# The last stage of an FNet + MLP kernel: two chunks multiplied, turned and stored by halves of rows

## The chip, the cores and the metric

The kernel runs on 1 core of one Trainium2 chip. The metric is the device time of one execution in microseconds (us), the median of several runs. TensorE (PE) multiplies into PSUM, VectorE (DVE) adds and turns 32x32 blocks, ScalarE (ACT) copies and applies functions, GpSimd (POOL), SyncE (SP) and ACT issue the transfers (DMAs).

## The reference: a Fourier mixing layer and an MLP, added

```python
xn = _layernorm(x, axis=-1)                     # x: 1 x 2048 x 640, fp32
a = einsum("bsd,ed->bse", xn, dft_hid_re)       # hidden DFT, 640 x 640
b = einsum("bsd,ed->bse", xn, dft_hid_im)
y = einsum("ts,bse->bte", dft_seq_re, a) - einsum("ts,bse->bte", dft_seq_im, b)   # 2048 x 2048
h = gelu(einsum("bsd,df->bsf", xn, w1) + b1)    # 640 -> 1536
out = x + y + einsum("bsf,fd->bsd", h, w2) + b2
```

All inputs and the output are fp32.

## The kernel before

**Arithmetic.** Each fp32 operand is split into a high and a low part, and `product` (L297) makes one product of three matmuls: high by high (L300), high by low (L301), low by high (L302). A matmul takes a 128x128 weight block and 512 moving columns and adds into one PSUM bank of 128 partitions by 512 columns. There are eight banks in one tensor, `banks`. The large products are done by a seven-product scheme of the Winograd kind, whose partial sums are kept in PSUM and in SBUF.

**Stages.** The MLP comes first, then the Fourier part. There the 2048 rows are four blocks of 512 (`TB`), and the sequence DFT is applied before the hidden one. Stages are walked in a list (L1691 to 1715). An "s" stage applies the sequence DFT to one block and leaves sums `u`, `u1`, `u2`, `v`, `v1`, `v2` in SBUF. After two such blocks, ta and tb, a "y" stage (`hidden_entry`, L1645, and `hidden_beside`, L1510) multiplies the sums of the pair by the pieces of the hidden DFT matrix. The last pair is ta = block 1 and tb = block 2, and `last` is true in its stage.

**The entries of a "y" stage.** It has 21 entries, n = 0 to 20: seven products w, each in three parts u (pieces 0 and 1, 2 and 3, 4 of the 640 long sum). For each entry the loop writes down, in this order, the matmuls (`hidden_entry`), what must stand ahead (`pre`), the splitting of the moving operand of entry n + 3 (`form`: the high part on ACT at L186, the low part on DVE at L189), and the work listed for n in `post`. Each engine works through its own instructions in that order; the framework puts in the waits between engines. A semaphore of a finished transfer is used again for a later one, eight of them in turn for SP and ACT together and eight for POOL, and a later transfer is issued when the earlier one of its semaphore has landed.

**Columns.** 640 output columns are four groups q of 160 (`DQ`), one in each quarter of the partitions. Each 160 are five chunks of 32 (`B`). Columns 0 to 63 of a group come first, 64 to 127 from banks X and X+1 last (`k` = 2 and 3 at the end of the kernel), 128 to 159 are the odd chunk. A bank holds a chunk turned round: it is transposed in 32x32 blocks by DVE and added to what the MLP left (`turned`, L1295, then `add_turned`, L1305, whose adds are recorded at L463). `store` (L1276) writes a stretch of columns of a block to the output with four transfers, one for each q, in turn on the queues that it is given.

**The end of the last pair.** Product w = 6 (entries 18 and 19) first finishes bank VS with 15 matmuls, then adds to bank X with 15 and to bank X+1 with 15. Beside it, DVE does in this order: at n = 17 `v1` (reads banks X and X+1, 1024 columns), the two steps of `yb2` (turn `v1`, add it into `u2`'s place, store columns 64 to 127 of tb on SP and ACT), and `end`, which adds a turned chunk of the MLP's result (`last_columns`, L1575, made at n = 2) into bank X+1 only; at n = 18 `yb4` (turn bank VS, add, store columns 128 to 159 of tb on POOL). After the loop (L1718 to 1725) chunk 2 of ta is turned out of bank X into SBUF, added and stored on SP and ACT, and then chunk 3 is turned out of bank X+1 straight into the output tile (L1722) and stored likewise.

Of the kernel before, what the change touches and what calls it, by code (L numbers as in the profile page):

```python
# [17 lines left out]
B = 32  # L18
# [8 lines left out]
def kernel(  # L27
# [88 lines left out]
    def bank(k):  # L116
        return banks[:, k]
# [80 lines left out]
    def rows_of(ap, t):  # L198
        return ap[t * TB : (t + 1) * TB].rearrange("(n r) d -> r n d", r=B)
# [97 lines left out]
    def product(acc, wsp, msp, first, last, goes_on=False):  # L297

        (wh, wl), (mh, ml) = wsp, msp
        nc.tensor.matmul(acc, wh, mh, start=first, stop=False, skip_group_check=goes_on)  # L300
        nc.tensor.matmul(acc, wh, ml, start=False, stop=False, skip_group_check=goes_on)  # L301
        nc.tensor.matmul(acc, wl, mh, start=False, stop=last, skip_group_check=goes_on)  # L302
# [159 lines left out]
    def add(dst, a, b, op=ALU.add):  # L462
        nc.vector.tensor_tensor(dst, a, b, op=op)  # L463
# [809 lines left out]
            for k in names:  # L1273
                nc.sync.dma_start(part_of(t, k), sums[t, k])

    def store(t, src, c0, c1, *queues):  # L1276

        queues = queues or (nc.sync,)
        for q in range(Q):
            queues[q % len(queues)].dma_start(  # L1280
                rows_of(out, t)[:, :, q * DQ + c0 : q * DQ + c1], src[q * B : (q + 1) * B]
            )

    def reload(lo, w, which="xab"):
# [33 lines left out]
    turn(2, 1)  # L1318
    build(len(builds) - 1, "c")

    def use(acc, w, lo, a, c, first, last, goes_on=False):
        cols = slice(lo * P, (lo + 1) * P)
        product(acc, (w[:, 0, cols], w[:, 1, cols]), (a[:, 0, c % 2], a[:, 1, c % 2]), first, last, goes_on)

    X, Y, Z, US, VS = 0, 3, 5, 2, 7
    yo = {}
# [1 line left out]
    def beside(h, t, n):  # L1328
# [108 lines left out]
        else:  # L1437
# [15 lines left out]
            if n == 6 and p == 2:  # L1453
# [4 lines left out]
                        nc.sync.dma_start(yo[t][:, :, c0:c1], ys[k][t])  # L1458

                post.append(load_yo)  # L1460
            if n == 6 and second:

                def load_y4():
                    yo[t, 4] = A["y4"](f"y4_{t}")
                    nc.sync.dma_start(yo[t, 4], ys[2][t])

                post.append(load_y4)
# [24 lines left out]
    def load_g(b, i):  # L1492
        if i >= NW * ND:
            return
        w, c = G[i]
        n = GWIDE[w] * P
        places = A["g", b]
        k = i % len(places)
        if b < len(blocks) - 1 and w == NW - 1:


            k = (i - 2 if c == CHUNKS[1][0] else i) % len(places)
            if c in CHUNKS[0]:
                k = CHUNKS[0].index(c)
                places = {k: fr_tile((P, 6 * P), f"u{2 - k}_{sets[blocks[b]]}", f"gr{k}_{b}", F32R)}
        g = places[k][:, : 2 * n].rearrange("p (a b) -> p a b", a=2)
        GT[b, i] = g
        nc.sync.dma_start(g.bitcast(F32), wits[w][c])

    def hidden_beside(b, n):  # L1510
# [8 lines left out]
        def s(which, k):  # L1519
            return sums[(ta, tb)[which], k]  # L1520
# [20 lines left out]
        def to(dst, acc, name, then=lambda: None):  # L1541


            def f():
                add_turned(dst, turned(acc, name))
                then()

            return f
# [21 lines left out]
            return f  # L1570

        def out_b(k):
            return lambda: store(tb, columns(k), 2 * k * B, 2 * (k + 1) * B, *(((nc.gpsimd,), (nc.sync, nc.scalar))[k] if last else ()))

        def last_columns():  # L1575

            A["end"] = A["rt2"][:, 0, 0, 0]
            nc.vector.transpose(A["end"].rearrange("p (n i) -> p n i", i=B), ya[:, :, 3 * B : 4 * B])

        yb1, yb2 = in_two(0), in_two(1)  # L1580
        yb4 = to(yo[tb, 4], vs, f"yb4_{tb}", lambda: store(tb, yo[tb, 4], 4 * B, DQ, *((nc.gpsimd,) if last else ())))
# [63 lines left out]
    def hidden_entry(n, b, w, u):  # L1645
        last = b == len(blocks) - 1
        where = (X, Y, Z, X, Z, X, X)[w]

        def use_g(acc, j, pos, first, stop, goes_on=False):
            r, k = (n - u + (pos // 2)) % 3, pos % 2  # L1650
            a = A["as"][:, r]
            use(acc, GT[b, w * ND + pos], j, a, k, first, stop, goes_on)

        def wide(j, pos):
            use_g(bank(where + j), j, pos, w < 3 and pos == 0, pos == ND - 1, w > 2)

        mine = (2 * u, 2 * u + 1) if u < 2 else (4,)
        if w == 6 and last:

            if u == 0:  # L1660
                for pos in range(ND):
                    use_g(bank(VS), 2, pos, False, pos == ND - 1)
                for pos in range(ND):
                    wide(0, pos)
            elif u == 1:
                for pos in range(ND):
                    wide(1, pos)
# [24 lines left out]
    for kind, what in stages:  # L1692
# [20 lines left out]
            X, Y, Z = Y, Z, X  # L1713
        if kind == "y":
            put_off.clear()


    t = blocks[-2][1]  # L1718
    for k in (2, 3):
        d = yo[t][:, :, k * B : (k + 1) * B]  # L1720
        if k == 3:
            nc.vector.transpose(d, bank(X + 1).rearrange("p (n i) -> p n i", i=B))  # L1722
# [34 lines left out]
```

## Time and profile before

| what | value |
|---|---|
| median of 3 runs (lowest to highest) | 852.09 us (851.99 to 852.13) |
| span of the profiled execution, first to last instruction | 849.9 us |
| instructions | 10599 |
| mean granted TensorE clock | 0.998 |
| PE, DVE, ACT, POOL busy | 841.9, 686.7, 368.6, 67.7 us |
| DMA | 166.53 MB, mean 196 GB/s |

The profiled execution is told of by its span alone; the three times are of other executions and lie 2.2 us above it, which is what stands outside the first and the last instruction. Times in the views count from the start of the span. In a timeline row stand the start, the duration, the engine, the line of the kernel, the operation, what is written and read, the shape and a count; "q" behind an engine means that its sequencer issues a transfer, and a bracket tells how long the engine had been idle and what ended that. "PEld" is the weight load of a matmul. The end of a matmul is modelled.

### The profile page before, as it was taken

The page shows a single profiled execution, that of the slowest core. Times are in us where ns is not written, and L with a number is a line of the kernel's source. Part 1 is how long each engine was busy: PE and PEld are TensorE (multiplying, and loading weights), DVE is VectorE, ACT ScalarE, POOL GpSimd, SP SyncE. Part 2 cuts the span into 40 slices and gives each one's busy share as a digit, 9 for nine tenths or more (in the row PEclk, how much of TensorE's full clock was granted, in tenths as well). Part 3 has the DMA queues.
Part 4 walks back from the last instruction along what each step waited for, and adds up shares of the span by engine and source line. Part 5 has one row for each costly group of instructions (what it writes and reads, how often), then busy time and mean ns, then how long its engine had stood idle before and what let it go on. Part 6 is the DMA issues. An engine that isn't in the chain of part 4 may idle for free.

```text
span 849.9 us, 10599 instructions
## 1 busy us (share of the span) xinstructions
PE 841.9 (99%) x3711; PEld 696.7 (82%) x3711; DVE 686.7 (81%) x909; ACT 368.6 (43%) x527; POOL 67.7 (8%) x116
## 2 busy tenths in 40 slices
PE   8999999999999999999999999999999999999997
PEld 7888888888888888888888888888888888888886
DVE  7979889767844778979978887889967998885687
ACT  7655666654453555443444344232323433323241
POOL 0440024222301000000000000000000000000002
PEclk9999999999999999999999999999999999999999
DMA  8995667878977897958744679763745799705464
GB/s 230 288 248 158 139 163 250 260 223 305 262 192 199 333 323 138 209 120 193 158 137 107 167 220 283 165 144 99 214 150 156 229 237 234 303 19 180 124 172 108
DMA packets 199141, 166.53 MB, mean 196 GB/s; under 512 B 61648, under 2 KB 170192, under 8 KB 198576
## 3 DMA queue, kind: packets, MB, share of 16 engines
q1 hardware_dynamic: 188320, 140.42, 62.7%
q0 software_dynamic: 7600, 24.91, 8.7%
q10 hardware_dynamic: 3168, 0.52, 0.3%
q8 instruction: 29, 0.48, 0.2%
q14 instruction: 24, 0.20, 0.1%
HBM read 115.75 MB, written 46.14 MB: 190 GB/s over the span
## 4 chain that ended last, share of the span: by engine, by line
PE 98%; DMA 1%; DVE 0%; ACT 0%; SPq 0%; issue 0%; ACTq 0%
PE banks L301 29%; PE banks L302 29%; PE banks L300 29%; PE banks L320 10%; DMA row<-in_A_x_dram 1%; PE banks L682 0%; DVE st L215 0%; ACT xp L714 0%; SPq L208 0%; DVE yo L1722 0%; DVE mv L216 0%; ACT mv L707 0%; DVE mv L708 0%; ACTq L707 0%
## 5 line engine op out<-in xcount | busy, mean ns | idle before, releaser
L186 ACT ACTIVATE as<-r 128x1024 fp32r<-128x1024 f32 x80 | 85.0, 1062 | 171.1 <-PE banks L302 150.4
L300 PE MATMUL banks<-as,xab 128*128 128x512 f32 x407 | 158.3, 389 | 0.0
L302 PE MATMUL banks<-as,xab 128*128 128x512 f32 x407 | 158.3, 389 | 0.0
L301 PE MATMUL banks<-as,xab 128*128 128x512 f32 x407 | 158.3, 389 | 0.0
L189 DVE TENSOR_TENSOR as<-r,as 128x1024 fp32r<-128x1024 f32 x80 | 97.2, 1215 | 38.1 <-ACT as L186 38.0
L301 PEld LDWEIGHTS banks<-as,xab 128*128 128x128 f32 x407 | 76.4, 188 | 15.9
L302 PEld LDWEIGHTS banks<-as,xab 128*128 128x128 f32 x407 | 76.4, 188 | 15.8
L300 PEld LDWEIGHTS banks<-as,xab 128*128 128x128 f32 x407 | 76.4, 188 | 15.8
L300 PE MATMUL banks<-as,xc 128*128 128x512 f32 x224 | 87.1, 389 | 0.0
L301 PE MATMUL banks<-as,xc 128*128 128x512 f32 x224 | 87.1, 389 | 0.0
L302 PE MATMUL banks<-as,xc 128*128 128x512 f32 x224 | 87.1, 389 | 0.0
L186 ACT ACTIVATE as<-rt 128x1024 fp32r<-128x1024 f32 x32 | 34.0, 1063 | 72.5 <-PE banks L302 57.9
L320 PE MATMUL banks<-xt,xab 128*128 128x512 f32 x240 | 56.8, 390 | 0.0
L189 DVE TENSOR_TENSOR hs<-ab,hs 128x512 fp32r<-128x512 f32 x36 | 24.7, 685 | 37.6 <-ACT hs L186 37.6
L320 PEld LDWEIGHTS banks<-xt,xab 128*128 128x128 f32 x240 | 45.0, 188 | 9.4
L301 PEld LDWEIGHTS banks<-as,xc 128*128 128x128 f32 x224 | 42.1, 188 | 8.8
L302 PEld LDWEIGHTS banks<-as,xc 128*128 128x128 f32 x224 | 42.0, 188 | 8.7
L300 PEld LDWEIGHTS banks<-as,xc 128*128 128x128 f32 x224 | 42.1, 188 | 8.7
L1280 POOL DMA_DIRECT2D out_dram<-u x4 | 2.6, 658 | 568.8 <-DVE u L463 568.8
L302 PE MATMUL banks<-hs,xc 128*128 128x512 f32 x120 | 46.7, 389 | 0.0
L300 PE MATMUL banks<-hs,xc 128*128 128x512 f32 x120 | 46.7, 389 | 0.0
L301 PE MATMUL banks<-hs,xc 128*128 128x512 f32 x120 | 46.7, 389 | 0.0
(240 smaller groups left out, 1678.9 us busy)
## 6 DMA issues: line engine op xcount, KB each, us to landing
raw<-in_A_dft_seq_re_dram SPq DMA_DIRECT2D x64, 256.0 KB, 5.4
raw<-in_A_dft_seq_im_dram SPq DMA_DIRECT2D x64, 256.0 KB, 5.1
w1r<-in_B_w_dram SPq DMA_DIRECT2D x144, 80.0 KB, 3.5
wit<-wst POOLq DMA_DIRECT2D x15, 384.0 KB, 4.2
wit<-wst POOLq DMA_DIRECT2D x20, 256.0 KB, 4.5
forms_ab<-xab SPq DMA_DIRECT2D x4, 1280.0 KB, 7.7
xab<-wit SPq DMA_DIRECT2D x13, 384.0 KB, 4.5
row<-xn SPq DMA_DIRECT2D x14, 320.0 KB, 5.3
```

Of the source, the lines that this page charges most:

```text
L186: nc.scalar.activation(h, s, AF.Copy)
L189: nc.vector.tensor_tensor(l, s, h.bitcast(F32), op=ALU.subtract)
L300: nc.tensor.matmul(acc, wh, mh, start=first, stop=False, skip_group_check=goes_on)
L301: nc.tensor.matmul(acc, wh, ml, start=False, stop=False, skip_group_check=goes_on)
L302: nc.tensor.matmul(acc, wl, mh, start=False, stop=last, skip_group_check=goes_on)
L320: nc.tensor.matmul(acc, W1[i][:, a, j * P : (j + 1) * P], XT[j][:, b], start=n == 0, stop=n == len(steps) - 1)
L1280: queues[q % len(queues)].dma_start(rows_of(out, t)[:, :, q * DQ + c0 : q * DQ + c1], src[q * B : (q + 1) * B])
```

## The change

It concerns the last pair alone. The last product of banks X and X+1 is done for columns 0 to 255 of both banks (rows 0 to 255 of the block) in entry 18, then for columns 256 to 511 of both in entry 19: 60 matmuls of 256 moving columns where there were 30 of 512. The MLP's chunks 2 and 3 are both turned ahead (`last_columns`, now 1024 wide) and both added in PSUM by `end`, which now stands right behind `v1`. Nothing is added behind the turning: `finish_part` turns the first half of both banks at once (entry 18), then the second half of bank X and the second half of bank X+1 (entry 19), each into the output tile, and stores its rows with four transfers on SP and ACT. For tb, columns 64 to 159 are gathered in one place, `end_b` (its last 32 columns loaded at n = 1 by `open_end`, in a place that was loaded with `load_y4` before), and stored by `yb4` with four transfers on SP and ACT in place of two stores of four.

```diff
-    def store(t, src, c0, c1, *queues):
+    def store(t, src, c0, c1, *queues, rows=slice(None)):
...
-                rows_of(out, t)[:, :, q * DQ + c0 : q * DQ + c1], src[q * B : (q + 1) * B]
+                rows_of(out, t)[:, rows, q * DQ + c0 : q * DQ + c1], src[q * B : (q + 1) * B]
...
-            if n == 6 and second:
+            if n == 6 and p == 1:
                 def load_y4():
...
         def columns(k):
+            if last and k:
+                return A["end_b"][:, :, : 2 * B]
...
         def out_b(k):
+            if last and k:
+                return lambda: None
...
         def last_columns():
-            A["end"] = A["rt2"][:, 0, 0, 0]
-            nc.vector.transpose(A["end"].rearrange("p (n i) -> p n i", i=B), ya[:, :, 3 * B : 4 * B])
+            A["end"] = A["rt2"][:, 0, 0]
+            nc.vector.transpose(
+                A["end"].rearrange("p e (n i) -> p e n i", i=B),
+                ya[:, :, 2 * B : 4 * B].rearrange("p n (e i) -> p e n i", i=B),
+            )
+        def open_end():
+            t = A["rt2"][:, 1].rearrange("p a b c -> p (a b c)")
+            A["end_b"] = t[:, : 3 * NB * B].rearrange("p (n e) -> p n e", n=NB)
+            yo[tb, 4] = A["end_b"][:, :, 2 * B :]
+            nc.sync.dma_start(yo[tb, 4], ys[2][tb])
...
+        def out_b4():
+            if last:
+                store(tb, A["end_b"], 2 * B, DQ, nc.sync, nc.scalar)
...
-        end = lambda: add(bank(X + 1), bank(X + 1), A["end"])
+        end = lambda: add(x_, x_, A["end"])
...
-            1: [f5s[1]],
+            1: [open_end] if last else [f5s[1]],
...
-            17: [v1, yb2, yb2, end] if last else [yb1, yb2],
-            18: [yb4] if last else [yb2],
-            19: [f6s[0]],
+            17: [v1, end, yb2, yb2] if last else [yb1, yb2],
+            18: [yb4, lambda: finish_part(0, 0, 2)] if last else [yb2],
+            19: [lambda: finish_part(1, 0, 1), lambda: finish_part(1, 1, 2)] if last else [f6s[0]],
...
             if u == 0:
                 for pos in range(ND):
                     use_g(bank(VS), 2, pos, False, pos == ND - 1)
-                for pos in range(ND):
-                    wide(0, pos)
-            elif u == 1:
-                for pos in range(ND):
-                    wide(1, pos)
+            if u < 2:
+                for j in range(2):
+                    for pos in range(ND):
+                        wide(j, pos, slice(u * TB // 2, (u + 1) * TB // 2))
...
+    def finish_part(u, j0, j1):
+        t, n0, n1 = blocks[-2][1], u * NB // 2, (u + 1) * NB // 2
+        cols = slice(u * TB // 2, (u + 1) * TB // 2)
+        d = yo[t][:, n0:n1, (2 + j0) * B : (2 + j1) * B]
+        nc.vector.transpose(
+            d.rearrange("p n (e i) -> p e n i", i=B),
+            banks[:, X + j0 : X + j1, cols].rearrange("p e (n i) -> p e n i", i=B),
+        )
+        store(t, d, (2 + j0) * B, (2 + j1) * B, nc.sync, nc.scalar, rows=slice(n0, n1))
...
-    t = blocks[-2][1]
-    for k in (2, 3):
-        d = yo[t][:, :, k * B : (k + 1) * B]
-        if k == 3:
-            nc.vector.transpose(d, bank(X + 1).rearrange("p (n i) -> p n i", i=B))
-        else:
-            add_turned(d, turned(bank(X), f"yt_{k}"))
-        store(t, d, k * B, (k + 1) * B, nc.sync, nc.scalar)
```

More of the change, by code (lines that the diff above doesn't have):

```diff
@@ L1319, with use @@
     build(len(builds) - 1, "c")
-    def use(acc, w, lo, a, c, first, last, goes_on=False):
+    def use(acc, w, lo, a, c, first, last, goes_on=False, part=slice(None)):
         cols = slice(lo * P, (lo + 1) * P)
-        product(acc, (w[:, 0, cols], w[:, 1, cols]), (a[:, 0, c % 2], a[:, 1, c % 2]), first, last, goes_on)
+        moving = a[:, 0, c % 2, part], a[:, 1, c % 2, part]
+        product(acc, (w[:, 0, cols], w[:, 1, cols]), moving, first, last, goes_on)
     X, Y, Z, US, VS = 0, 3, 5, 2, 7
@@ L1572, in out_b, with yb4 @@
         def out_b(k):
-            return lambda: store(tb, columns(k), 2 * k * B, 2 * (k + 1) * B, *(((nc.gpsimd,), (nc.sync, nc.scalar))[k] if last else ()))
+            if last and k:
+                return lambda: None
+            return lambda: store(tb, columns(k), 2 * k * B, 2 * (k + 1) * B, *((nc.gpsimd,) if last else ()))
         def last_columns():
-            A["end"] = A["rt2"][:, 0, 0, 0]
-            nc.vector.transpose(A["end"].rearrange("p (n i) -> p n i", i=B), ya[:, :, 3 * B : 4 * B])
-        yb1, yb2 = in_two(0), in_two(1)
-        yb4 = to(yo[tb, 4], vs, f"yb4_{tb}", lambda: store(tb, yo[tb, 4], 4 * B, DQ, *((nc.gpsimd,) if last else ())))
+            A["end"] = A["rt2"][:, 0, 0]
[8 more added lines that the diff above has]
+            nc.sync.dma_start(yo[tb, 4], ys[2][tb])
+        yb1, yb2 = in_two(0), in_two(1)
+        def out_b4():
+            if last:
+                store(tb, A["end_b"], 2 * B, DQ, nc.sync, nc.scalar)
+            else:
+                store(tb, yo[tb, 4], 4 * B, DQ)
+        def yb4():
+            to(yo[tb, 4], vs, f"yb4_{tb}", out_b4)()
         f5s = [lambda u=u: f5(u) for u in range(2)] if not last else [lambda: None] * 2
@@ L1647, in hidden_entry, with use_g, wide @@
         where = (X, Y, Z, X, Z, X, X)[w]
-        def use_g(acc, j, pos, first, stop, goes_on=False):
+        def use_g(acc, j, pos, first, stop, goes_on=False, cols=slice(None)):
             r, k = (n - u + (pos // 2)) % 3, pos % 2
             a = A["as"][:, r]
-            use(acc, GT[b, w * ND + pos], j, a, k, first, stop, goes_on)
-        def wide(j, pos):
-            use_g(bank(where + j), j, pos, w < 3 and pos == 0, pos == ND - 1, w > 2)
+            use(acc, GT[b, w * ND + pos], j, a, k, first, stop, goes_on, cols)
+        def wide(j, pos, cols=slice(None)):
+            use_g(bank(where + j)[:, cols], j, pos, w < 3 and pos == 0, pos == ND - 1, w > 2, cols)
         mine = (2 * u, 2 * u + 1) if u < 2 else (4,)
```

## The prediction

> **What bounds the kernel now.** I read the page first, then the timeline of the last 16 us by engine, then the DMA share behind the last matmul.
>
> ```profile
> span 849.9 us, 10599 instructions
> PE 841.9 (99%) x3711; PEld 696.7 (82%) x3711; DVE 686.7 (81%) x909; ACT 368.6 (43%) x527; POOL 67.7 (8%) x116
> PE 98%; DMA 1%; DVE 0%; ACT 0%; SPq 0%; issue 0%; ACTq 0%
> ```
>
> PE is busy for 99% of the span, and the chain that ended last is PE. So the change can move only two things: the time of the last matmul, and the stretch behind it. The timeline of the end:
>
> ```profile
> 834.31 1.82 DVE L189 TENSOR_TENSOR as<-v,as 128x1024 fp32r<-128x1024 f32 x2
> 836.05 1.22 DVE L463 TENSOR_TENSOR v<-v,banks 128x1024 f32<-128x1024 f32 x1
> 837.30 1.25 DVE L1302 STREAM_TRANSPOSE yb<-v 128x1024 f32<-128x1024 f32 x1
> 837.61 0.39 PE L300 MATMUL banks<-as,xab 128*128 128x512 f32 x1
> 838.58 1.23 DVE L463 TENSOR_TENSOR u<-u,yb 128x1024 f32<-128x1024 f32 x1
> 839.72 0.69 DVE L463 TENSOR_TENSOR banks<-banks,rt 128x512 f32<-128x512 f32 x1
> 839.83 0.95 ACTq L1280 DMA_DIRECT2D out_dram<-u  x2
> 840.32 0.70 DVE L1299 STREAM_TRANSPOSE yb<-banks 128x512 f32<-128x512 f32 x1
> 841.01 0.39 PE L300 MATMUL banks<-as,xab 128*128 128x512 f32 x1
> 841.06 0.69 DVE L463 TENSOR_TENSOR y<-y,yb 128x512 f32<-128x512 f32 x1
> 841.86 0.72 DVE L1299 STREAM_TRANSPOSE yt<-banks 128x512 f32<-128x512 f32 x1
> 843.33 3.35 ACTq L1280 DMA_DIRECT2D out_dram<-yo  x4
> 844.18 0.39 PE L302 MATMUL banks<-as,xab 128*128 128x512 f32 x1
> 844.61 0.72 DVE L1722 STREAM_TRANSPOSE yo<-banks 128x512 f32<-128x512 f32 x1 [1.31 <-PE banks L302]
> ```
> ```profile
> 845.35 1.33 ACTq L1280 DMA_DIRECT2D out_dram<-yo  x2
> ```
> ```profile
> 845.77 0.92 ACTq L1280 DMA_DIRECT2D out_dram<-yo  x1
> ```
>
> Bank X gets its last product from 837.61 on, bank X+1 from 841.01 on, and the last of the 30 matmuls starts at 844.18: 6.57 us in 29 steps, 0.227 a step. It ends at 844.57. DVE turns bank X+1 from 844.61 to 845.33, the first two of four transfers are issued at 845.35, the fourth at 845.77, and the span ends at 849.9. So 5.3 us lie behind the last matmul: 0.78 to the first issue, 0.42 to the fourth, 4.1 from there.
>
> Note also DVE: from 834.31 to 842.6 it goes without a pause, and `v1` (836.05 to 837.27) reads banks X and X+1 just 0.34 us before PE writes bank X again.
>
> **The change part by part.**
>
> *1. `end` is widened and put ahead of bank X: +1.0 us.* Before, `end` touched bank X+1 alone, at 839.72, 0.6 us before PE came to it. Now it adds to both banks and must be done before the first matmul on X. It can start only behind `v1`, at 837.25. A 1024-wide add with a PSUM operand took 1.22 (`v1`), so it ends at 838.47, where PE is ready at 837.61: 0.86 us. To this I add 0.05 from engine to engine (844.57 to 844.61 above) and 0.11 for a first weight load with no matmul to hide it (below): PE starts at 838.63, 1.02 late. Nothing stands behind these matmuls on PE that could fill the hole. Below this it can't be, unless DVE reaches `v1` sooner, and what stands ahead of `v1` isn't changed.
>
> *2. 60 matmuls of 256 columns for 30 of 512: +0.4 us.* No matmul of 256 columns is in the trace. The nearest rows are from the kernel's start, and the weight loads of the end:
>
> ```profile
> 9.71 2.27 PE L682 MATMUL banks<-ident,xp 128*128 128x128 f32 x19 [0.73 <-ACT xp L714]
> ```
> ```profile
> 12.05 0.30 PEld L320 LDWEIGHTS banks<-xt,xab 128*128 128x128 f32 x2
> ```
> ```profile
> L301 PEld LDWEIGHTS banks<-as,xab 128*128 128x128 f32 x11 | 2.1, 188 | 0.4
> ```
>
> A weight load is recorded with 188 ns, and each matmul has its own. If the next matmul could only start when that is over, the step would be 0.19 and the upper bound 60 x 0.19 = 11.4 us for the 6.8 of now. But two such loads stand together in 0.30 us, so that the second began 0.11 to 0.12 after the first, and 19 turning matmuls of 128 columns came (2.27 - 0.27) / 18 = 0.111 apart. The lower bound is half of today's step, 0.113. I take 0.12, nearest to the pair of loads: 7.2 for 6.8.
>
> In the Trainium skill, "TensorE: Matmul & The Clock Gate", section "Back-to-back issue gap", the warm gap is the columns over 2.4 plus 2.5 ns, 109 ns for 256 columns. An estimate by it is 60 x 0.109 = 6.5 us, 0.7 less than my term, and a sum of 852.5; but for 512 columns it says 216 ns, where this trace shows 227.
>
> *3. Half 0 is turned before half 1 is multiplied: +1.1 us.* `finish_part(0, 0, 2)` reads columns 0 to 255 of both banks and stands in program order ahead of the matmuls that write columns 256 to 511 of the same banks. The trace has no PE write and DVE access on one bank at once: `v1` on X and X+1 ends before 837.61, `end` on X+1 ends at 840.41 before 841.01, and each turning follows its bank's last matmul. So the bounds are nothing (if the halves count as apart) and a full wait. I take the wait, since every use of these banks in the rows above is one after the other. PE is through with half 0's starts at 838.63 + 30 x 0.12 = 842.23, its last result is there at 842.39 (a recorded 0.39 less the 0.11 of 256 columns not streamed, 0.28, from its start). Is DVE free? Behind `end` stand `yb2` (1.25 and 1.23) and `yb4` (0.70 and 0.69), at the spacing of today's rows until 842.3: just. The turning of 128x512 out of PSUM takes 0.72, until 843.15, and PE goes on at 843.31 instead of 842.23.
>
> In the Trainium skill, "PSUM — Partial Sum Buffer", section "PSUM bank collisions raise a hardware error", two engines must be kept off one bank and quarter of the partitions at once, disjoint columns included. By it the wait has to be there, and the sum is mine; no row here shows such an overlap either way.
>
> The last matmul then starts at 843.31 + 29 x 0.12 = 846.79 and ends at 847.07, 2.5 us later than the 844.57 of now (1.0 + 0.4 + 1.1).
>
> *4. Behind the last matmul: -1.4 us.* What is left is a turning of 128x256. 512 took 0.72 and 1024 took 1.25, 0.53 for 512 more, so 256 are about 0.45: -0.27. The four issues are as before. Then the landing:
>
> ```profile
> 845.00:846.00 1.00, 0.00 (x0) 0.00 (x0) 0.32 (x1) 0.00 (x0) 0.00 (x0) 1.00 1.01 191
> 847.00:848.00 1.00, 0.00 (x0) 0.00 (x0) 0.00 (x0) 0.00 (x0) 0.00 (x0) 0.50 1.21 189
> 848.00:849.00 1.00, 0.00 (x0) 0.00 (x0) 0.00 (x0) 0.00 (x0) 0.00 (x0) 0.50 0.12 17
> ```
> ```profile
> out_dram<-yo ACTq DMA_DIRECT2D x4, 64.0 KB, 3.0
> ```
> ```profile
> DMA to landing us min/median/max: 2.0/3.3/6.7
> ```
>
> The DMA engines are full (share 1.0 and more) until 848, because chunk 2's transfers, issued at 843.33, and POOL's of `y` still run when chunk 3's come. The stores of `yo` land 3.0 after their issue, while the least of all stores at this line is 2.0. After the change the last four are 32 KB each, not 64, and the big ones were issued 4 to 5 us ahead (`end_b`, 4 x 192 KB, at 842.35; half 0, 4 x 64 KB, at 843.2) and 2 us ahead (the first 4 x 32 KB). I take 2.0 for 3.0 and, as the transfers are half as large, 0.1 more: -1.1. The bounds are 0 and -1.2. Together the end behind the last matmul is 5.3 - 1.4 = 3.9 us.
>
> *5. What costs nothing.*
>
> ```profile
> 794.86 0.70 DVE L1578 STREAM_TRANSPOSE rt<-yo 128x512 f32<-128x512 f32 x1
> 798.75 1.23 DVE L189 TENSOR_TENSOR as<-u,as 128x1024 fp32r<-128x1024 f32 x1 [3.19 <-ACT as L186]
> ```
> ```profile
> L1465 SPq DMA_DIRECT2D y<-ys x1: 320/320/320, 725.4 to 725.4; - x1
> ```
> ```profile
> 824.88 2.59 SPq L1536 DMA_DIRECT2D u<-ys  x2
> ```
> ```profile
> 784.00:790.00 6.00, 6.00 (x29) 4.95 (x28) 2.16 (x3) 1.06 (x1) 0.00 (x0) 1.00 0.27 87
> ```
>
> The wider `last_columns` is 0.5 us more of DVE ahead of 3.19 us of idling; without that cover it would delay the splitting at L189. The load of `end_b` moves from 725.4 into the stage, among SP's loads of matrix pieces, at a DMA share of 0.27, and PE is busy all of that window; it could only cost if a piece came late, and then some 2 us of transfer at most. `load_yb(1)`, the second at 824.88 + 2.3, now writes short stretches; its data are first needed at 840.9. The stores of `end_b` leave POOL for SP and ACT, where at 842.35 nothing else waits but the stores of `finish_part`.
>
> **Sum:** +1.0 + 0.4 + 1.1 - 1.4 = +1.1 us on the span of 849.9. The median stands 2.2 above that, and nothing of the change lies there: 852.1 + 1.1 = **853.2 us**. That is 0.13%, within the 0.2% (1.7 us: 850.4 to 853.8) that a measurement of this kernel can tell from no change.
>
> **The rivals.**
>
> *A: no wait between the halves.* Then term 3 falls away and the last matmul ends at 845.99. But not all of the 1.1 comes back: the last transfers would then be issued at 846.5 into engines that still carry `end_b`. I put it at 852.5 (852.1 to 853.0). For it speaks that the columns are disjoint; against it that the trace shows only use after use.
>
> *B, the other side, slower: the weight load bounds the narrow matmul.* Its place is the 60 matmuls, its price is 60 x (0.19 - 0.12) = 4.2 us, so 857.4; it makes the kernel slower by over 0.2% from a step of 0.13 on (60 x 0.01 = 0.6 above my sum). For it: the recorded 188 ns. Against it: the two loads in 0.30 us.
>
> *C: the last stores wait for earlier ones.* Behind 842 there are now sixteen transfers on SP and ACT, and eight semaphores; the ninth to sixteenth each wait until the one eight before has landed.
>
> ```profile
> SPq L208 <- DMA w2r<-in_B_w_dram: 1.5, 2, 1.2
> out_dram<-u ACTq DMA_DIRECT2D x1, 128.0 KB, 4.0
> ```
>
> The first row shows such a wait: a load of x held by the landing of a weight, up to 1.2 us. Four transfers of 128 KB took up to 4.0 to land. If those of 192 KB take 4.5, the fourth (issued 842.8) is in at 847.3, ACT's last but one issue of the first small four follows, and the last four slip by 0.3 to 0.9: 853.8 (853.5 to 854.3). In my sum they land in time by some tenths.
>
> *D: the change is as good as it can be:* neither wait of terms 1 and 3, and the shorter end: 852.1 + 0.4 - 1.4 = 851.1. Against it stands the DVE row of `v1`.
>
> **How the numbers follow.** My sum 0.50, A 0.15, B 0.10, C 0.20, D 0.05. My own case spans 852.7 to 853.7 (a step of 0.113 takes 0.4 off, half of the gain in landing adds 0.5). The range reaches from A's low part to C's high end, 851.9 to 854.3, and leaves out B and D. Faster by over 0.2% would need 850.4, below even D: 0.02. Slower takes B, half of C and a little of my own case's upper end: 0.22. Within: 0.76.
>
> **What would show it.** Right: DVE's 1024-wide add on `banks` right behind `v1`, PE idle for about 1 us before its first 256-column matmul near 838.6 and again for about 1 us between its 30th and 31st; a step of 0.12 among them; a last turning of 0.45; a last store landing about 2 us after its issue. Wrong: a step of 0.19 (B), no second hole (A), or the last issues more than 0.1 behind the last turning, held by a landing (C). The prediction as a whole fails if DVE reaches `v1` much later or earlier than 836, since terms 1 and 3 both hang on it.

## The result and the profile after

| | before | after |
|---|---|---|
| median of 10 runs each, same chip (lowest to highest) | 851.93 us (851.33 to 852.75) | 854.28 us (853.28 to 856.23) |
| span of the profiled execution | 849.9 us | 852.5 us |
| start of `v1` | 836.05 | 836.40 |
| start of `v1` to the end of the last matmul | 8.52 | 10.93 |
| from there to the landing of the last store | 4.40 | 3.46 |
| from there to the end of the span | 0.97 | 1.65 |

The ratio is 1.0027 (95% interval 1.0019 to 1.0035): the change makes the kernel slower by 2.35 us. That is inside the range on record, by 0.02 us at its upper end of 854.3, and 1.1 us above its likeliest value; it is just beyond the 0.2% that the prediction took for no change, and the 853.8 of rival C came nearest. The median of after lies 1.8 above its profiled span and that of before 2.0 above its own, so the spans carry the difference.

DVE's rows of the timeline after, beside the rows of the end that the prediction shows of before:

```profile
836.40 1.22 DVE L463 TENSOR_TENSOR v<-v,banks 128x1024 f32<-128x1024 f32 x1
837.53 1.23 DVE L463 TENSOR_TENSOR banks<-banks,rt 128x1024 f32<-128x1024 f32 x1
...
842.02 0.69 DVE L463 TENSOR_TENSOR rt<-rt,yb 128x512 f32<-128x512 f32 x1
842.71 0.72 DVE L1718 STREAM_TRANSPOSE yo<-banks 128x512 f32<-128x512 f32 x1
845.58 0.45 DVE L1718 STREAM_TRANSPOSE yo<-banks 128x256 f32<-128x256 f32 x1 [2.15 <-PE banks L302]
847.38 0.45 DVE L1718 STREAM_TRANSPOSE yo<-banks 128x256 f32<-128x256 f32 x1 [1.34 <-PE banks L302]
```

PE's rows around the two places where it stops, and its last matmul:

```profile
837.73 0.39 PE L302 MATMUL banks<-as,xab 128*128 128x512 f32 x1
838.81 0.39 PE L300 MATMUL banks<-as,xab 128*128 128x256 f32 x1 [0.70 <-DVE banks L463]
839.04 0.28 PE L301 MATMUL banks<-as,xab 128*128 128x256 f32 x1
```
```profile
842.39 0.28 PE L302 MATMUL banks<-as,xab 128*128 128x256 f32 x1
843.48 0.39 PE L300 MATMUL banks<-as,xab 128*128 128x256 f32 x1 [0.81 <-DVE yo L1718]
843.70 0.28 PE L301 MATMUL banks<-as,xab 128*128 128x256 f32 x1
```
```profile
847.06 0.28 PE L302 MATMUL banks<-as,xab 128*128 128x256 f32 x1
```

Read the brackets: the first names the wide add into the banks, the second the turning of half 0, and from one start to the next there are 1.09 us in both places (837.73 to 838.81, 842.39 to 843.48). Within a half, 28 steps from 839.04 or 843.70 to the 30th matmul take 3.35 and 3.36 us, 0.120 each. The last matmul ends at 847.34, and behind it come the stores. The issues of SP and ACT, and the DMA share by stretches:

```profile
842.74 0.87 SPq L1280 DMA_DIRECT2D out_dram<-rt  x2
843.70 5.64 SPq L1280 DMA_DIRECT2D out_dram<-yo  x6
842.74 0.95 ACTq L1280 DMA_DIRECT2D out_dram<-rt  x2
843.78 5.81 ACTq L1280 DMA_DIRECT2D out_dram<-yo  x6
```
```profile
844.00:845.00 1.00, 1.00 (x10) 1.00 (x10) 0.00 (x0) 0.00 (x0) 0.00 (x0) 1.00 0.88 213
845.00:846.00 1.00, 1.00 (x11) 1.00 (x10) 0.42 (x1) 0.00 (x0) 0.00 (x0) 1.00 0.93 221
846.00:847.00 1.00, 1.00 (x11) 1.00 (x10) 0.03 (x1) 0.00 (x0) 0.00 (x0) 1.00 0.95 233
847.00:848.00 1.00, 0.34 (x3) 0.13 (x2) 0.45 (x1) 0.00 (x0) 0.00 (x0) 1.00 1.00 220
848.00:849.00 1.00, 0.00 (x0) 0.00 (x0) 0.00 (x0) 0.00 (x0) 0.00 (x0) 1.00 1.04 184
849.00:850.00 1.00, 0.00 (x0) 0.00 (x0) 0.00 (x0) 0.00 (x0) 0.00 (x0) 1.00 0.72 118
```
```profile
out_dram<-rt SPq DMA_DIRECT2D x2, 192.0 KB, 3.5
out_dram<-rt ACTq DMA_DIRECT2D x2, 192.0 KB, 4.1
out_dram<-yo SPq DMA_DIRECT2D x2, 64.0 KB, 4.3
out_dram<-yo ACTq DMA_DIRECT2D x2, 64.0 KB, 4.4
out_dram<-yo SPq DMA_DIRECT2D x4, 32.0 KB, 2.0
out_dram<-yo ACTq DMA_DIRECT2D x4, 32.0 KB, 1.7
```

The second column from the right is the share of the DMA engines: 0.88 to 1.04 for five microseconds. The 768 KB of `end_b` go out from 842.74 on, and behind them half 0's four stores of 64 KB take 3.9 to 4.9 us to land (the table has the medians of SP's and ACT's), although they are issued from 843.70 to 845.24, over 3 us ahead of the last ones. Their issues alone took 1.4 to 1.65 us each. The last turning is done at 847.83, but the last four stores are issued at 848.52, 848.75, 849.01 and 849.24, each within 0.1 us of the landing of one of half 0's stores (848.46, 848.68, 848.99, 849.22), whose semaphore it uses again. So the last stores were held up by the landings of the stores ahead of them. (Single landings and semaphore numbers stand in the trace's own records; the views print only sums of them.)

The last store lands at 850.80, and the span still goes on for 1.65 us, where the kernel before needs 0.97. Behind the last landing SP goes through a row of waits, one for each semaphore, in the order 101, 103, 105, 106, 107, 108, 109, 110. In the kernel before, the store that lands last carries 109, and one more wait remains behind it. After the change it carries 105: five remain at about 0.06 us each, and 0.33 us pass between two closing instructions that lie 0.05 apart before; what the second of them waits for the trace doesn't tell.

### The profile page after: what moved, and what is told of

It reads as the page before. It is cut to its first block, busy times and chain, and to the rows that moved or that the text cites. A ratio compares the mean times of both kernels' runs of the same rounds, so it can differ in the third digit from the quotient of the medians.

```text
span 852.5 us, 10659 instructions
## 1 busy us (share of the span) xinstructions
PE 841.8 (99%) x3741; PEld 697.7 (82%) x3741; DVE 687.5 (81%) x909; ACT 368.5 (43%) x527; POOL 65.2 (8%) x112
## 4 chain that ended last, share of the span: by engine, by line
PE 97%; DVE 2%; issue 0%; ACT 0%; DMA 0%; SPq 0%; DVEq 0%
PE banks L300 29%; PE banks L301 29%; PE banks L302 29%; PE banks L320 10%; DVE as L189 1%; PE banks L666 0%; DVE v L463 0%; PE banks L682 0%; DVE rt L463 0%; DMA w1r<-in_B_w_dram 0%; DVE yb L1302 0%; SPq L278 0%; DVE yo L1718 0%; DVE u L463 0%; ACT as L186 0%
## 5 line engine op out<-in xcount | busy, mean ns | idle before, releaser
L300 PE MATMUL banks<-as,xab 128*128 128x512 f32 (+1 forms) x417 | 160.3, 384 | 1.5 <-DVE yo L1718 0.8
L302 PE MATMUL banks<-as,xab 128*128 128x512 f32 (+1 forms) x417 | 160.1, 384 | 0.0
L301 PE MATMUL banks<-as,xab 128*128 128x512 f32 (+1 forms) x417 | 160.1, 384 | 0.0
L300 PEld LDWEIGHTS banks<-as,xab 128*128 128x128 f32 x417 | 78.4, 188 | 17.6 <-DVE banks L463 1.1
L301 PEld LDWEIGHTS banks<-as,xab 128*128 128x128 f32 x417 | 78.4, 188 | 15.6
L302 PEld LDWEIGHTS banks<-as,xab 128*128 128x128 f32 x417 | 78.4, 188 | 15.4
```

## The experiments

The experiments asked which of these waits and stores cost the time.

**Theory.** Up to the last matmul the terms of the prediction hold: two waits of PE for DVE, and narrow matmuls at 0.12. Behind it the gain of 1.4 us was not had, since `end_b`'s 768 KB, sent at once ahead of the last stores, fill the engines, and since the closing row takes 0.7 longer. **Rivals:** the holes are worth less than they look, since an earlier last matmul only meets the same stores; the queue and its semaphores hold up the last stores, and not the bytes; the closing stretch has nothing to do with the semaphores.

All runs have 5 rounds against the kernel before on the same chip. In the table, a is the time from the start of `v1` to the end of the last matmul, b from there to the last landing, c from there to the end of the span, and d the sum's excess over the kernel before (13.89). All four are of the profiled execution. They begin at `v1`, so that what goes on earlier is left out. In the kernel after and in the five that change only its stores (e4, e5, e7, e8, e9), a comes out at 10.93 or 10.94 each time. The ratios are coarser: the intervals of two that differ by less than 0.001 overlap.

| kernel | a | b | c | d | median (before, same chip) | ratio, interval |
|---|---|---|---|---|---|---|
| before | 8.52 | 4.40 | 0.97 | 0 | | |
| after | 10.93 | 3.46 | 1.65 | 2.16 | 854.28 (851.93) | 1.0027, 1.0019 to 1.0035 |
| e1_end_narrow | 10.43 | 3.54 | 1.65 | 1.73 | 853.59 (851.50) | 1.0021, 1.0012 to 1.0030 |
| e2_turn_behind | 9.86 | 5.20 | 0.98 | 2.14 | 853.68 (851.50) | 1.0024, 1.0014 to 1.0034 |
| e3_full_width | 9.51 | 5.59 | 0.98 | 2.19 | 853.58 (851.64) | 1.0024, 1.0015 to 1.0033 |
| e4_stores_apart | 10.93 | 2.76 | 1.65 | 1.45 | 852.99 (851.50) | 1.0017, 1.0008 to 1.0026 |
| e5_no_end_b_store | 10.94 | 2.73 | 0.97 | 0.74 | 852.57 (851.50) | 1.0012, 1.0003 to 1.0021 |
| e7_end_b_on_pool | 10.93 | 4.43 | 0.97 | 2.43 | 853.92 (851.66) | 1.0028, 1.0017 to 1.0039 |
| e8_apart_turned | 10.93 | 2.71 | 1.00 | 0.75 | 854.98 (851.64) | 1.0040, 1.0027 to 1.0052 |
| e9_u1_on_sp_act | 10.93 | 3.39 | 1.36 | 1.79 | 855.55 (851.64) | 1.0046, 1.0034 to 1.0059 |
| b1_end_alone | 9.51 | 4.00 | 0.97 | 0.58 | 852.14 (851.66) | 1.0006, 0.9998 to 1.0015 |
| f1_y_on_sp_act | 8.54 | 4.33 | 1.65 | 0.64 | 852.27 (851.66) | 1.0006, 0.9997 to 1.0014 |
| f2_last_turned_in_two | 8.54 | 4.55 | 1.06 | 0.27 | 851.84 (851.66) | 1.0002, 0.9994 to 1.0011 |
| f3_f1_turned_round | 8.46 | 4.33 | 1.31 | 0.20 | 854.30 (851.64) | 1.0032, 1.0021 to 1.0042 |

The last column in us (1.0027 is 2.3) agrees with d within 0.3 in all rows but e8, e9 and f3, of which more below.

### The matmuls: e1, b1, e2, e3

**e1_end_narrow:** the wide add made 512 columns wide, on bank X+1 alone; chunk 2 goes without the MLP's share.

```diff
-        end = lambda: add(x_, x_, A["end"])
+        end = lambda: add(bank(X + 1), bank(X + 1), A["end"][:, 1])
```

> The changed kernel, but `end` adds to bank X+1 alone, as before the change; chunk 2 of the last pair lacks the MLP's share. Theory (the two holes hang together through DVE's queue): the first hole of PE goes (about 1.0 us), but DVE reaches the turning of half 0 only 0.5 us earlier, so the second hole grows from 0.8 to about 1.3; the last matmul comes 0.5 earlier, the end behind it stays at 5.1, and the time is about 0.5 us less than the changed kernel's. Rival (the holes are independent): 1.0 us less, second hole still 0.8.

The first hole is gone (the first narrow matmul starts at 837.71, 0.23 behind the matmul before it), but the second takes more:

```profile
842.76 0.39 PE L300 MATMUL banks<-as,xab 128*128 128x256 f32 x1 [1.30 <-DVE yo L1718]
```

From the matmul before it are now 1.58 us instead of 1.09: counted from `v1`, PE is through with half 0 1.0 sooner than in the kernel after, but DVE, whose add is 0.5 shorter, comes to the turning only 0.5 sooner. Of the first hole only 0.5 is had, in a as in the ratio. The theory, that both holes hang on one queue of DVE, holds.

**b1_end_alone:** the kernel before with the wide add behind `v1` and nothing else of the change; `last_columns` turns both chunks ahead as in the change, and chunk 2 is then turned without an add (these two edits are left out here).

```diff
-            17: [v1, yb2, yb2, end] if last else [yb1, yb2],
+            17: [v1, end, yb2, yb2] if last else [yb1, yb2],
...
-        end = lambda: add(bank(X + 1), bank(X + 1), A["end"])
+        end = lambda: add(x_, x_, A["end"])
```

> The kernel before with one part of the change: both chunks turned ahead and both added in PSUM by `end` right behind `v1`; matmuls of 512 columns and stores as before, nothing added behind the turning of chunk 2. Theory: one hole of PE of about 1.1 us ahead of bank X, so the last matmul 1.1 later; chunk 2 is out a little earlier than before against the last matmul, so chunk 3's transfers meet emptier queues and the end behind it shrinks from 5.4 to 4.4 to 4.9; in all 0.3 to 0.6 us slower than the kernel before. Rival (the end behind the last matmul doesn't depend on the stores ahead of it): 1.1 slower.

The one hole is there again (the bracket below), and a grows by 0.99, term 1 as forecast. But 0.4 of it comes back in b, so that 0.58 is left. Two things help there: the earlier stores have had longer to drain before chunk 3's, and chunk 2's, which no add holds up, start 0.3 sooner (6.96 behind `v1` for 7.28). The run does not part them.

```profile
838.53 0.50 PE L300 MATMUL banks<-as,xab 128*128 128x512 f32 x1 [0.67 <-DVE banks L463]
```

**e2_turn_behind:** all four turnings of 256 columns stand behind the last product in the program, so that nothing reads the banks between the halves.

```diff
-            18: [yb4, lambda: finish_part(0, 0, 2)] if last else [yb2],
-            19: [lambda: finish_part(1, 0, 1), lambda: finish_part(1, 1, 2)] if last else [f6s[0]],
+            18: [yb4] if last else [yb2],
+            19: [lambda j=j, u=u: finish_part(u, j, j + 1) for j in range(2) for u in range(2)] if last else [f6s[0]],
```

> The changed kernel, but the turning of half 0 stands behind the matmuls of half 1 in program order, and each of the four half chunks is turned and stored by itself. Theory (the second hole is a wait of PE for the turning of the same banks, put in because the turning stands first): no hole between the 30th and 31st narrow matmul, the last matmul 1.0 to 1.1 us earlier; behind it stand two turnings of 0.45 and twenty transfers share eight semaphores, so the end behind it grows from 5.1 to 5.5 or 6; in all 0.2 to 0.7 us less than the changed kernel. Rival (PE waits there for something else, such as its operands): the hole stays and the time is the same or longer.

PE goes through the halves without a stop, with one hole left, and a is 1.07 less: the second hole is the wait for the turning, and rival A (no wait between the halves) is out. The 1.07 are given back behind the last matmul, where b is 5.20: twelve of sixteen stores of 32 KB are issued only there (845.99 to 848.91). Of the 0.2 to 0.7 us that were expected, d shows 0.02 and the ratio 0.3, which its interval can't tell from nothing.

In the Trainium skill, "PSUM — Partial Sum Buffer", section "PSUM bank collisions raise a hardware error", disjoint columns of a bank do not free two engines from each other. The 1.09 us of the kernel after agree with it, though what is seen is a wait that the framework put in, and not what would happen without it.

**e3_full_width:** the two chunks at 512 columns again, chunk 2 turned and stored by halves beside chunk 3's matmuls, chunk 3 by halves behind them (entries 18 and 19 list the turnings accordingly).

```diff
-                for j in range(2):
-                    for pos in range(ND):
-                        wide(j, pos, slice(u * TB // 2, (u + 1) * TB // 2))
+                for pos in range(ND):
+                    wide(u, pos)
```

> The kernel after with chunks 2 and 3 multiplied at their full width of 512 columns, chunk 2 turned and stored by halves while chunk 3 is multiplied, and chunk 3 by halves behind its last matmul; the wide add ahead of bank X and everything else as in the kernel after. Theory: the second hole (1.1 us, the wait for a turning that reads the same banks) and the 0.4 us of 60 narrow matmuls go: 9.4 to 9.5 us from v1 to the last matmul's end instead of 10.9, and one hole of 1.1 us. Two turnings of 0.45 us stand behind the last matmul instead of one, and the same stores have 1.5 us less to drain: the stretch behind it grows by 0.4 to 0.9 us, to 5.5 to 6.0; sum 0.6 to 1.1 us under the kernel after, ratio 1.0014 to 1.0020. Rival, the stores that have to drain at the end set it whatever the matmuls do: all of the 1.5 us is given back, ratio 1.0026.

As the theory had it, a is 1.42 less (term 3 and term 2 gone). As the rival had it, nothing of this reaches the end: b and c make 6.57 instead of 5.12, and d is that of the kernel after. The last issues are at 849.15 to 849.89, 3.2 to 3.9 us behind the last matmul's end at 845.96; the queues are busy until then:

```profile
846.91 3.18 SPq L1280 DMA_DIRECT2D out_dram<-yo  x6
846.98 3.37 ACTq L1280 DMA_DIRECT2D out_dram<-yo  x6
```

So in the kernel after, two chains end nearly together, the matmuls and the stores that start with `end_b`; the matmuls shortened alone gain nothing in e2 and e3. (It isn't a clean cut: there are sixteen stores of 32 KB here, four more than in the kernel after.)

### The stores: e4, e5, e7

**e4_stores_apart:** tb's last 96 columns stored as before the change, 64 when `yb2` is done, on SP and ACT, and 32 on POOL.

```diff
-            if last and k:
-                return lambda: None
-            return lambda: store(tb, columns(k), 2 * k * B, 2 * (k + 1) * B, *((nc.gpsimd,) if last else ()))
+            return lambda: store(tb, columns(k), 2 * k * B, 2 * (k + 1) * B, *(((nc.gpsimd,), (nc.sync, nc.scalar))[k] if last else ()))
...
-                store(tb, A["end_b"], 2 * B, DQ, nc.sync, nc.scalar)
+                store(tb, yo[tb, 4], 4 * B, DQ, nc.gpsimd)
```

> The changed kernel, but block 2's last 96 columns are stored as before: 64 columns behind `yb2` on SP and ACT, 32 behind `yb4` on POOL; same bytes. Theory (the one late store of 768 KB fills the queues of SP and ACT, so that half 0's stores take 1.4 to 1.6 us to issue and the last eight wait for landings): half 0's issues take 0.4 each, the last four start within 0.1 of the last turning and its neighbours, the end behind the last matmul is 4.0 to 4.4 instead of 5.1, and the time 0.7 to 1.1 us less than the changed kernel's. Rival (the bytes set the end, whichever queue carries them): within 0.3 of the changed kernel.

**e5_no_end_b_store:** no store of these 96 columns at all; the output lacks them.

> The changed kernel without the four transfers of block 2's last 96 columns (they are left out of the output). Theory: nothing is in the way of the last stores, the end behind the last matmul is 3.9 us, as the prediction's fourth term had it, and the time is 1.2 us less than the changed kernel's. Rival (the end is set by issue and landing of the last small stores alone, whatever stands ahead): within 0.3 of the changed kernel.

**e7_end_b_on_pool:** `end_b` whole, but on POOL's queue.

```diff
-                store(tb, A["end_b"], 2 * B, DQ, nc.sync, nc.scalar)
+                store(tb, A["end_b"], 2 * B, DQ, nc.gpsimd)
```

> The changed kernel, but the late store of block 2's 96 columns is issued by POOL instead of SP and ACT: same bytes, same moment, its own queue and semaphores. Theory (the last stores are held in the queues and by the semaphores of SP and ACT behind that store): half 0's issues take 0.3 to 0.5 each, the last four start right behind the last turning, the end behind the last matmul is 4.3 to 4.6 and the time 0.6 to 0.8 us less than the changed kernel's. Rival (768 KB so late keep the DMA engines full, whoever issues them): the last issues are early but land 3 or more later, the end stays at 5 or so.

The landing times of the three, from the table of issues in the last 10 us, e5 first, then e4, then e7:

```profile
out_dram<-yo SPq DMA_DIRECT2D x2, 64.0 KB, 1.8
...
out_dram<-yo SPq DMA_DIRECT2D x4, 32.0 KB, 1.6
```
```profile
out_dram<-rt SPq DMA_DIRECT2D x2, 128.0 KB, 3.5
...
out_dram<-rt POOLq DMA_DIRECT2D x4, 64.0 KB, 3.2
out_dram<-yo SPq DMA_DIRECT2D x2, 64.0 KB, 2.8
...
out_dram<-yo SPq DMA_DIRECT2D x4, 32.0 KB, 2.0
```
```profile
out_dram<-rt POOLq DMA_DIRECT2D x4, 192.0 KB, 4.6
out_dram<-yo SPq DMA_DIRECT2D x2, 64.0 KB, 3.2
...
out_dram<-yo SPq DMA_DIRECT2D x4, 32.0 KB, 3.6
```

Without the 768 KB the end behind the last matmul is 3.70 us, where the prediction's term 4 has 3.9; the fourth of the last issues stands 0.93 behind the last matmul there, for 1.90 in the kernel after. With the same bytes, but the first 512 KB sent when they are ready (issued at 840.36 in e4, where `v1` starts 0.83 sooner than in the kernel after and `end_b` there only at 842.74), b is 2.76, nearly as without them. On POOL's queue nothing is better: the small stores take 3.6 us, their issues up to 1.7, and b is 4.43. My theory for this run, that it is the queue of SP and ACT with its semaphores, fell. So it is the late bytes that cost the time, whichever queue carries them; the semaphore is only where the wait shows. (e4 moves two things, the time of the first 512 KB and the queue of the last 256 KB. That the queue alone doesn't help is e7's; the two are not parted further.)

### The closing row: f1, f2, e8, e9, f3

**f1_y_on_sp_act:** the kernel before, with the store of tb's last 32 columns on SP and ACT instead of POOL. **f2_last_turned_in_two:** the same, with chunk 3 turned and stored in two halves behind its matmuls.

```diff
-        yb4 = to(yo[tb, 4], vs, f"yb4_{tb}", lambda: store(tb, yo[tb, 4], 4 * B, DQ, *((nc.gpsimd,) if last else ())))
+        yb4 = to(yo[tb, 4], vs, f"yb4_{tb}", lambda: store(tb, yo[tb, 4], 4 * B, DQ, *((nc.sync, nc.scalar) if last else ())))
```

> The kernel before with the store of block 2's last 32 columns issued by SP and ACT instead of POOL; none of the change. Theory (the end of the kernel before hangs on how early the bytes ahead of the last store leave): POOL's four issues of 0.65 each are replaced by pairs of 0.4, the DMA engines get those 256 KB up to 1.5 us earlier and chunk 3's transfers land 2.3 to 2.7 after their issue instead of 3.2; 0.3 to 0.8 us faster than the kernel before. Rival (semaphores and queues of SP and ACT become the hold, as in the changed kernel): same or slower.

> As the kernel before with block 2's last 32 columns stored by SP and ACT, and chunk 3 turned out of bank X+1 in two halves of 256 columns (both after its last matmul), each stored by itself with four transfers of 32 KB. Theory: the first half is issued 0.27 earlier, the second 0.1 later than the whole was; the transfers are as many bytes in twice as many issues, and the second four wait for their semaphores or queues, so within 0.3 of the same kernel with one turning. Rival (halves by rows pay by themselves): 0.3 or more faster than it.

f1 isn't faster, as its rival had it, but not for the rival's reason: its stores land as before (b 4.33 for 4.40), and what it loses is in c, 1.65 for 0.97, where the theory saw no change. In f2, b does not gain by the halves (4.55), and c is 1.06. In both, c goes with the semaphore of the last landing (105 in f1, 109 in f2), and so in all earlier runs: 105 in the kernel after, e1 and e4, with 1.65; 109 in before, e2, e3, e5, e7 and b1, with 0.97 or 0.98. To make this more than a coincidence, three kernels move it by four more transfers, far ahead of the end: u1's columns of tb on SP and ACT instead of POOL, in the kernel after (**e9_u1_on_sp_act**), in e4 (**e8_apart_turned**) and in f1 (**f3_f1_turned_round**). The new line is the same in all three; e9's edit:

```diff
-            return lambda: store(tb, columns(k), 2 * k * B, 2 * (k + 1) * B, *((nc.gpsimd,) if last else ()))
+            return lambda: store(tb, columns(k), 2 * k * B, 2 * (k + 1) * B, *((nc.sync, nc.scalar) if last else ()))
```

> The kernel after, with the four transfers of u1's columns (the last block's first 128 columns) put on SP's and ACT's queues instead of GpSimd's. They are issued some 15 us before the end and landed long before it. In the kernel after, 1.65 us pass from the last landing to the end of the span, in the kernel before 0.97; the semaphores of SP's and ACT's transfers come round after eight, and in the first case the transfer that lands last carries 105, in the second 109. Theory: the length of this stretch is set by where the last transfer's semaphore stands in SP's closing row of waits (101, 103, 105 and on to 110): four more transfers earlier move it by four, to 109, so 0.97 us instead of 1.65, and all else stays: two holes of 1.1 us, 10.9 us from v1 to the last matmul's end, 4.4 us behind the last matmul instead of 5.1, median 0.6 to 0.7 us under the kernel after, ratio 1.0019 (1.0016 to 1.0024). Rival, the stretch goes with something else (the size or the number of late transfers, which don't change here): 1.65 us and a ratio of 1.0027 remain. A second rival: the issues (some 0.4 us each, two on ACT) delay ACT's or SP's other work: the last matmul ends later.

> Both repairs of the end together: the other block's last 96 columns stored as before the change (64 at once on SP's and ACT's queues, 32 on GpSimd's), which took 0.85 us off the end in a run above, and u1's columns on SP's and ACT's queues, so that the transfer that lands last carries 109. Theory: 3.7 us behind the last matmul (2.76 to the last landing, 0.97 from there), so what term 4 of the prediction had at 3.9; the path to the last matmul's end stays at 10.9 us from v1; ratio 1.0009 (1.0004 to 1.0014), all of what is left from the two holes and the narrow matmuls. Rival, 1.65 us remain from the last landing to the end: 4.4 us, ratio 1.0017.

> The kernel before, with both the last block's last 32 columns and its first 128 on SP's and ACT's queues, none of the last stores on GpSimd's. With the 32 columns alone moved, a run above took 0.6 us more than the kernel before, with 1.65 us from the last landing to the end for 0.97. Four more transfers move the last one's semaphore back to a late place in the closing row. Theory: 0.97 us again, no hole, 5.3 us behind the last matmul, ratio 0.9999 (0.9995 to 1.0003): the move of the 32 columns itself gains nothing, and what it lost was the closing row. Rival, the stretch goes with the SP and ACT queues' late work: 1.65 us, ratio 1.0006.

The semaphore of the last landing is 109 in all three, and c falls to 1.00 in e8, but to 1.36 and 1.31 only in e9 and f3. There SP's row of waits is through 0.2 to 0.3 us behind the landing, as it is with 109 elsewhere, and the 0.3 that are over lie between the last two closing instructions (0.76 us for 0.46, from the end of the first to the end of the second); what they wait for there stays open. So the place of the last semaphore in the row is worth 0.3 to 0.65 us: the theory holds in its direction, and in e8 in its size.

The medians of all three are far worse, by the second rival that the first expectation named. In e8:

```profile
834.01 0.95 ACTq L1280 DMA_DIRECT2D out_dram<-u  x2
835.06 1.58 ACT L186 ACTIVATE as<-v 128x1024 fp32r<-128x1024 f32 x2 [4.12 <-issue]
```
```profile
836.16 0.50 PE L300 MATMUL banks<-as,xab 128*128 128x512 f32 x1 [0.89 <-ACT as L186]
837.43 0.50 PE L301 MATMUL banks<-as,xab 128*128 128x512 f32 x1 [0.76 <-DVE as L189]
```

u1's stores wait on ACT until DVE is done with them at 834; behind them on the same engine stands the splitting of the next moving operands, which in e4, the kernel without the move, goes ahead at its time:

```profile
832.54 1.07 ACT L186 ACTIVATE as<-v 128x1024 fp32r<-128x1024 f32 x1 [1.66 <-PE banks L302]
833.90 0.63 ACT L186 ACTIVATE as<-v 128x512 fp32r<-128x512 f32 x1 [0.29 <-PE banks L302]
```

In e8 it comes at 835.06, PE waits twice, and `v1` starts at 837.89. That is 2.3 us later than in e4 (835.57); so it is in e9 (838.66 for the 836.40 of the kernel after) and in f3 (837.88 for the 835.59 of f1). That is ahead of `v1` and so outside a to d.

No version beats the kernel before; f2 (1.0002), b1 and f1 (both 1.0006) can't be told from it, and e8's end, joined to a `v1` that is not delayed, would by d still be 0.75 behind.

## Why the prediction was right up to the last matmul, and 1.2 us short behind it

The time fell inside the range by 0.02 us. The sum was 1.1 too low, all of it behind the last matmul. The range had taken in rival C's price, and C was in part what happened; that it still held with the 0.68 of the closing row, which neither the sum nor a rival had, was luck. By the prediction's own signs its first three terms came out and its fourth did not: the last issues came 0.7 to 1.0 late, held by landings, which was to speak for C.

- **Term 1 (+1.0): right.** From `v1` to the first matmul on X are 2.41 us for 1.56, +0.85, and 0.11 for the first matmul behind the stop (0.23 to the next start): +0.96. That it costs much less at the end when it stands alone (b1, +0.58) was not foreseen: "Nothing stands behind these matmuls on PE that could fill the hole" was right for PE, and left out the stores, which drain meanwhile.
- **Term 2 (+0.4): right.** The step is 0.120: 59 of them and the 0.28 of the last matmul are 7.34, for 6.96 before (29 steps of 0.227 and 0.39), so +0.38. Rival B (0.19) is out: the weight loads are recorded at 0.19 each and start 0.12 apart. By the formula in the Trainium skill, "TensorE: Matmul & The Clock Gate", section "Back-to-back issue gap", it would have been 0.109. The measurement is 0.011 above it, as it is for 512 columns (0.227 against 0.216). The same section of the Trainium skill calls this formula the gap of an isolated matmul and gives about 0.131 for 512 columns in a stream of weight loads and matmuls. The 0.227 of this kernel, with its fp32r operands, does not bear that out.
- **Term 3 (+1.1): right.** 0.97 more than a step between the halves, and 0.11 for the first matmul: +1.08. Together +2.42 for the +2.5 on record.
- **Term 4 (-1.4): failed.** Measured: -0.25. The turning is 0.45 as forecast. The sum had the fourth issue 0.93 behind the last matmul, 2.0 to its landing and 0.97 to the end, 3.9. Measured are 1.90, 1.56 and 1.65, so +0.97, -0.44 and +0.68. The step that failed is "The four issues are as before": they waited for the landings of half 0's stores. "I take 2.0 for 3.0" held, and the landing was even shorter. The sum had the transfers ahead "land in time by some tenths", the big ones being issued "4 to 5 us ahead"; they were not gone by then. The working saw that 768 KB would be issued at 842.35 (842.74 measured, of which 0.35 is the later `v1`), and did not hold that against the 190 GB/s of its own DMA rows. An estimate by that rate: the 768 KB take 4.1 us, half 0's 256 KB 1.4 and the first small stores' 128 KB 0.7 more, until 848.6, a microsecond after the first of the last stores was due. e5, without these bytes, has the 0.93 to the fourth issue that the sum had, 1.79 to its landing and 0.97 to the end: 3.7.
- **Rival C: its place and its size were right,** its cause half. The last four issues slipped by 0.7 to 1.0 (0.3 to 0.9 expected), each released by a landing, and with the shorter landing this adds 0.53 to the sum, where C's 853.8 adds 0.6. But e7 shows that other semaphores and another queue for the big store don't help: the last issues slip there by 0.3 to 1.0, behind issues of up to 1.7 us.
- **The closing row (+0.68)** stands in no term. The prediction took the stretch from the last landing to the end as fixed. Without it the median would, by estimate, have been near 853.6.
- **Term 5: no cost seen** in the widened turning ahead and the moved load: `v1` starts at 835.53 to 836.44 in the seven kernels that have both and leave u1's stores on POOL, and at 835.59 to 836.48 in the three that have neither. But what its last sentence was to show did not follow: that `end_b`'s stores on SP and ACT find nothing else waiting is no reason that they cost nothing.

## What to carry to other kernels

Where a kernel ends in stores, draw up the last microseconds as bytes against the measured rate, and not as the latency of the last store: two stores gathered into one go out when the later one is ready, and hold up all behind them. A hole of TensorE near the end is worth less than its length, as long as stores ahead are still draining (0.58 of 0.99 in b1, and nothing of 1.07 in e2, which has four more stores). A store that waits on an engine's queue for data holds up that engine's own arithmetic behind it (2.3 us here for two transfers on ACT).

## What the runs showed of the hardware that was not expected

- Issuing a transfer on SP or ACT took 1.4 to 1.65 us each for the four behind 768 KB on their way, for 0.3 to 0.9 at the end of the kernel before and 0.3 to 0.5 in e5, without these bytes; POOL's transfers delay SP's and ACT's issues too (e7: up to 1.7).
- From the last landing to the end of the span it took 0.97 to 1.06 us in eight kernels where the last transfer's semaphore stood late in SP's closing row of waits, and 1.65 in the four where it stood early; two more with a late one took 1.31 and 1.36.
- 256-column matmuls of this kind come every 0.120 us, each with its own weight load of 0.19 recorded: the loads overlap.
